# Sinkhorn attention with a feed-forward layer: wider products, products of zeros, and a new order of calls for the first two chunks

## The chip, the cores and the metric

The kernel runs on one core of one Trainium2 chip. The metric is the device time of one launch in microseconds (us), lower is better. TensorE (PE in the profile) multiplies, VectorE (DVE), ScalarE (ACT) and GpSimd (POOL) do the rest, SyncE (SP) only issues transfers (DMAs); POOL and ACT issue some too.

## The reference

```python
P = sort_net                                   # batch 4, 8 heads, 8 x 8 blocks
for _ in range(5):                             # Sinkhorn
    P = exp(P - max(P, -1)); P = P / (sum(P, -1) + 1e-9); P = P / (sum(P, -2) + 1e-9)
k_sorted = einsum('bhij,bhjcd->bhicd', P, k_b) # blocks of 96 positions, head_dim 64
v_sorted = einsum('bhij,bhjcd->bhicd', P, v_b)
attn = softmax(q_b @ k_sorted^T / 8)           # 96 x 96 within each block
x = (attn @ v_sorted) with the heads side by side   # 3072 tokens x 512
h = x @ w_in                                   # 512 -> 2048
out = (h * cos(h)) @ w_out                     # 2048 -> 512
```

All inputs and the output are float32; the kernel multiplies in bfloat16.

## The kernel before

The 3072 tokens are eight chunks of 384: chunk `n` is half of batch `n // 2`, four blocks of 96 tokens numbered `u` = 0 to 3. For each chunk the kernel computes four score tiles (one for each `u`, eight heads), softmax, the products with the sorted V, a transpose to `xT`, and the two feed-forward products: `up` with cosine and gate, then `down`. Before that K and V are sorted: products of K and V with a block matrix made from `P` (`bds`, `bdv`).

Each engine runs its instructions in the order of the calls, so the order written out by hand at the end of the kernel sets everything. The work of chunk 0 and 1 and the sorting of the first batch's K and V are spread over one long list of calls to small helpers (L770 to L962). From chunk 2 on `moe_up` and `moe_down` take slots with calls.

PSUM has two pools: `B` (`big`, three buffers of two banks) and `C` (`acc`, two of one bank). A helper that takes a tile waits until an earlier tile's readers are done.

The helpers, by what they do. `kp`, `ks`: products that sort K (three and six tiles), `k_place`, `kse`: their copies out of PSUM. `v0(z)`: eight products that sort an eighth of V of batch 0, `v0e(z)` its copy; z from 4 on reads `vperm`, which GpSimd's `v_permute` fills in two copies, eighths 4 and 5 first. A product reads 128 columns of `vperm` where a channel has 96, so that the last product of `v0(5)` reads into the second copy. `s_ps`, `s_max`, `s_sub`, `expo`: a score tile, its maximum, the subtraction and the exponential. `p_ps`, `p_ev`: transposes of the exponentials and their copy. `av_products`, `av_norm`: products with V and the division. `x_ps`, `x_ev`: transposes to `xT`. `q_products`, `q_place_half`: transposes of Q. `up_four`, `cos_four`, `gate_four`, `down_four`, `down_out`: the feed-forward layer of chunk 0, over half of its tokens (`h`), four of 16 slices (`g`). `keep_warm(n, tile)`: n products of zeros into a tile that is overwritten afterwards; `idle(n)` the same into a tile of its own.

In `v0` each product has more columns than are kept, and the next overwrites the rest:

```python
w = 2 * NB if t == 7 else 4 * NB          # 64 or 128 columns
nc.tensor.matmul(o[:, t * 2 * NB:t * 2 * NB + w], v_cols(z * 8 + t, z > 3)[:64],
                 bdv[:64].rearrange("p x i -> p (x i)")[:, :w], start=True, stop=True)
```

In chunk 2 `expo(2, u)` sends its exponentials through a transposing DMA on SP's queue (unless told to leave that to PE), `down(n, ts, half, stores)` computes 128 tokens of the output in two halves of eight products, copies them to `o_s` and stores them, also through SP's queue. `p_hold(2, 2)` makes GpSimd wait for the transpose of tile (2, 2) before it issues further loads.

The order of calls before, L770 to L963 (several to a line):

```python
v_permute(slice(0, 64), D // 2, False); kp(0, *B); spread(bdv, blocks[1]); kp(2, *B); k_place(0, A); kp(1, *B)
k_place(2, V); v0(0, *C); k_place(1, A); v0(1, *C); v0e(0, V); s_ps(0, 0); v0e(1, A); v0(4, *B); s_max(0, 0)
s_ps(0, 2); load_w_out(0); v0e(4, A); load_w_out(1); load_w_out(2); load_w_out(3); v0(5, *C); ones(0); s_sub(0, 0)
v0(3, *C); v0e(5, A); s_max(0, 2); v0(6, *B); expo(0, 0, True); s_ps(0, 1); s_sub(0, 2); v0e(3, A); p_ps(0, 0, *C)
v0e(6, A); s_max(0, 1); v0(2, *B); p_ev(0, 0, A); s_sub(0, 1); s_ps(0, 3); kxp(1); v0e(2, A); s_max(0, 3)
expo(0, 1, True); v0(7, *B); kxp(0); v0e(7, A); s_sub(0, 3); p_ps(0, 1, *C); kxp(2); z_turned(1); expo(0, 2, True)
av_products(0, 0); p_ev(0, 1, V); expo(0, 3, True); av_norm(0, 0, True); p_ps(0, 2, *B); load(kbuf, 0, kin_d[1])
load(vbuf, 64, vin_d[1]); picks(pick_pair, (2, 3)); av_products(0, 1); p_ev(0, 2, A); p_ps(0, 3, *C)
av_norm(0, 1, True); x_ps(0, 0, *B); q_products(1, 1, 0, 16, *C); x_ev(0, 0, A); p_ev(0, 3, V); x_ps(0, 1, *B)
z_vperm(); av_products(0, 2); q_place_half(1, 1, 0, A); x_ev(0, 1, V); av_products(0, 3); av_norm(0, 2, True)
up_four(0, 0, 0); up_four(0, 0, 1); q_place_half(1, 1, 1, V); z_turned(0); p_pads(); up_four(0, 1, 0)
av_norm(0, 3, True); cos_four(0, 0); up_four(0, 1, 1); gate_four(0, 0); x_ps(0, 3, *C); x_ps(0, 2, *C); cos_four(0, 1)
up_four(0, 2, 0); x_ev(0, 3, V); up_four(0, 2, 1); x_ev(0, 2, A); gate_four(0, 1); up_four(1, 1, 0); cos_four(0, 2)
up_four(1, 1, 1); gate_four(0, 2); up_four(1, 2, 0); cos_four(1, 1); up_four(1, 2, 1); gate_four(1, 1)
up_four(1, 3, 0); cos_four(1, 2); up_four(1, 3, 1); gate_four(1, 2); up_four(1, 0, 0); cos_four(1, 3)
up_four(1, 0, 1); gate_four(1, 3); q_products(1, 0, 0, 16, *C); cos_four(1, 0); last = block(pick_pair, *C)
q_place_half(1, 0, 0, V); up_four(0, 3, 0); q_place_half(1, 0, 1, A); gate_four(1, 0); up_four(0, 3, 1); s_ps(1, 2)
spread(bds[1], last); cos_four(0, 3); s_ps(1, 0); s_max(1, 2); down_four(2, 0); load_q(2)
load_pair(pair, kin_d, 0 * CD // 2, 1 * CD // 2); load_pair(pair, kin_d, 1 * CD // 2, 2 * CD // 2); s_max(1, 0)
v_permute(slice(64, 128)); down_four(2, 1); down_four(2, 2); s_sub(1, 2); down_four(2, 3); gate_four(0, 3)
expo(1, 2, True); ks(2, *C); down_out(2, A); s_sub(1, 0); ks(1, *B); s_ps(1, 1); kse(2, A); p_ps(1, 2, *C)
s_max(1, 1); expo(1, 0, True); s_ps(1, 3); down_four(1, 0); p_ev(1, 2, V); kse(1, A); down_four(1, 1); s_sub(1, 1)
p_ps(1, 0, *B); s_max(1, 3); down_four(1, 2); p_ev(1, 0, A); s_sub(1, 3); av_products(1, 2); expo(1, 1, True)
down_four(1, 3); av_norm(1, 2, True); expo(1, 3, True); p_ps(1, 1, *B); av_products(1, 0); p_ev(1, 1, V)
down_out(1, A); x_ps(1, 2, *C); p_ps(1, 3, *B); av_norm(1, 0, True); x_ev(1, 2, A); av_products(1, 1); down_four(0, 0)
p_ev(1, 3, A); av_norm(1, 1, True); x_ps(1, 0, *C); av_products(1, 3); x_ev(1, 0, V); ks(4, *B); av_norm(1, 3, True)
x_ps(1, 1, *B); down_four(0, 1); x_ev(1, 1, A); kse(4, A); x_ps(1, 3, *B); down_four(0, 2); x_ev(1, 3, V)
down_four(0, 3); ks(0, *B); down_out(0, V); ks(3, *B); kse(0, A); ks(5, *B); kse(3, V); kse(5, A); k_swap(kT[1])
q_transpose(2, 0, (V, V), *B); q_transpose(2, 1, (V, V), *B); zeros_between(3)
```

## Time and profile before

| | |
|---|---|
| median of three runs | 242.27 us (242.16, 242.27, 243.8) |
| profiled execution, its own time | 242.27 us |
| span of its trace | 240.5 us |
| mean granted clock of PE | 0.972 |
| PE busy | 228.5 us (95%) |
| DVE, ACT, POOL busy | 171.8, 153.4, 93.7 us |
| DMA | 30.89 MB, mean 128 GB/s |

The span runs from the first to the last instruction; 1.77 us of the time lie around it. A busy PE is not a PE at its peak: the granted clock says how fast it ran. In the timeline, start and length come first, then engine, line, operation, tile written and tiles read, with the count of instructions; what stands in brackets is the idle time of the engine before it and what ended that. The chain of waits is followed back from the last instruction.

### The profile page before, as it was taken

The page shows a single profiled execution, that of the slowest core. Times are in us where ns is not written, and L with a number is a line of the kernel's source. Part 1 is how long each engine was busy: PE and PEld are TensorE (multiplying, and loading weights), DVE is VectorE, ACT ScalarE, POOL GpSimd, SP SyncE. Part 2 cuts the span into 40 slices and gives each one's busy share as a digit, 9 for nine tenths or more (in the row PEclk, how much of TensorE's full clock was granted, in tenths as well). Part 3 has the DMA queues.
Part 4 walks back from the last instruction along what each step waited for, and adds up shares of the span by engine and source line. Part 5 has one row for each costly group of instructions (what it writes and reads, how often), then busy time and mean ns, then how long its engine had stood idle before and what let it go on. Part 6 is the DMA issues. An engine that isn't in the chain of part 4 may idle for free.

```text
span 240.5 us, 5340 instructions
## 1 busy us (share of the span) xinstructions
PE 228.5 (95%) x2176; PEld 146.3 (61%) x2197; DVE 171.8 (71%) x285; ACT 153.4 (64%) x204; POOL 93.7 (39%) x117
## 2 busy tenths in 40 slices
PE   8888999999999979999999999999999999999993
PEld 3477899666765556655666465655664565456552
DVE  5668766996798656895578986997798769535700
ACT  3366766774889728888488847683767377546511
POOL 7699994893980068960724401700000000000000
PEclk9996579999999999999999999999999999999999
DMA  6999999893899659869798959924982460341012
GB/s 84 212 200 205 203 219 221 118 225 101 141 101 197 144 109 176 127 138 167 103 127 98 117 92 173 182 50 94 118 219 45 85 184 0 68 120 44 3 44 87
DMA packets 66423, 30.89 MB, mean 128 GB/s; under 512 B 55136, under 2 KB 61920, under 8 KB 66144
## 3 DMA queue, kind: packets, MB, share of 16 engines
q0 software_dynamic: 24048, 13.64, 41.3%
q1 hardware_dynamic: 42064, 16.73, 32.5%
q8 instruction: 17, 0.28, 0.5%
q10 hardware_dynamic: 288, 0.20, 0.3%
q14 instruction: 6, 0.05, 0.1%
HBM read 27.27 MB, written 6.29 MB: 140 GB/s over the span
## 4 chain that ended last, share of the span: by engine, by line
PE 74%; DMA 13%; ACT 4%; DVE 3%; POOL 3%; issue 2%; ACTq 0%; DVEq 0%; POOLq 0%
PE h L557 30%; PE o L582 18%; PE h L727 5%; DMA pT<-p_buf 5%; DMA kv<-in_v_dram 5%; PE o L748 4%; PE av L513 3%; PE sc L406 3%; DMA vperm<-p_buf 2%; POOL vperm L179 2%; PE vs L660 2%; PE pps L705 2%; PE ks L376 1%; ACT p_buf L468 1%; DVE s L450 1%
## 5 line engine op out<-in xcount | busy, mean ns | idle before, releaser
L557 PE MATMUL h<-xT,w_in_t 128*128 128x384 bf16 x448 | 78.4, 326 | 0.0
L582 PE MATMUL o<-w_out_t,gg 128*128 128x512 bf16 x303 | 73.6, 379 | 0.9
L565 DVE TENSOR_TENSOR gg<-c,h 128x768 bf16<-128x768 f32 x56 | 52.6, 949 | 18.8 <-ACT c L561 18.8
L561 ACT ACTIVATE c<-h,half_pi 128x768 f32<-128x768 f32 x56 | 50.4, 900 | 22.0 <-PE h L557 21.2
L557 PEld LDWEIGHTS <-w_in_t 128*128 128x128 bf16 x448 | 42.3, 98 | 26.1 <-issue 0.2
L582 PEld LDWEIGHTS <-gg 128*128 128x128 bf16 x320 | 29.0, 98 | 27.6
L179 POOL COPY vperm<-kv 64x1536 bf16<-64x1536 bf16 (+1 forms) x10 | 28.2, 2858 | 0.8 <-DMA kv<-in_v_dram 0.8
L468 ACT ACTIVATE p_buf<-s 96x768 bf16<-96x768 f32 x32 | 25.9, 839 | 2.0 <-DMA pT<-p_buf 0.8
L450 DVE TENSOR_TENSOR s<-sc,mx 96x384 f32<-96x384 f32 (+1 forms) x33 | 24.3, 735 | 1.8
L448 DVE TENSOR_REDUCE mx<-sc 96x4 f32<-96x384 f32 (+1 forms) x33 | 24.1, 729 | 0.7 <-PE sc L406 0.7
L526 DVE TENSOR_TENSOR xn<-av,r 96x512 bf16<-96x512 f32 x32 | 22.0, 687 | 1.1
L524 DVE RECIPROCAL r<-av 96x8 f32<-96x8 f32 x32 | 6.4, 199 | 14.3 <-PE av L513 14.1
L129 POOL DMA_DIRECT2D kv<-in_q_dram x24 | 15.9, 674 | 0.8 <-issue 0.5
L249 ACT CAST kTs<-ks 128x512 bf16<-128x512 f32 (+1 forms) x19 | 11.6, 627 | 7.1 <-PE ks L376 7.1
L406 PE MATMUL sc<-kTs,q_turned 128*128 128x96 bf16 x224 | 15.4, 206 | 0.0
L406 PEld LDWEIGHTS <-q_turned 128*128 128x128 bf16 x224 | 12.7, 98 | 3.6 <-DVE s L450 0.4
L249 ACT COPY kv<-o 128x512 f32<-128x512 f32 x8 | 4.7, 582 | 12.5 <-PE o L582 12.5
L727 PE MATMUL h<-xT,w_in_t 128*128 128x192 bf16 x128 | 12.1, 259 | 0.0
L238 PE MATMUL idle<-warm 128*128 128x512 bf16 x28 | 9.4, 486 | 2.5 <-ACT q_turned L321 1.5
L727 PEld LDWEIGHTS <-w_in_t 128*128 128x128 bf16 x128 | 11.4, 104 | 0.1
L748 PE MATMUL o<-w_out_t,gg 128*128 128x512 bf16 x45 | 11.4, 379 | 0.2
L249 ACT COPY o_s<-o 128x512 f32<-128x512 f32 (+2 forms) x10 | 5.3, 530 | 9.6 <-PE o L582 6.4
(114 smaller groups left out, 282.7 us busy)
## 6 DMA issues: line engine op xcount, KB each, us to landing
...
```

The source lines that it names most:

```text
L179: nc.gpsimd.tensor_copy(dst, src)
L249: eng.copy(dst, src)
L406: nc.tensor.matmul(out, q_of(n, hp)[:, x:x + 128], keys_of(n, u, h2, hp), start=True, stop=True)
L448: nc.vector.reduce_max(mx[:], scv, axis=AX.X)
L450: nc.vector.tensor_tensor(s, scv, mx.to_broadcast(list(s.shape)), op=ALU.subtract)
L468: nc.scalar.activation(p[:, :, :blk], s_t.pop((n, u)).rearrange("p e h c -> p (e h) c"), AF.Exp, scale=scale)
L526: nc.vector.tensor_tensor(xn.rearrange("p h e d -> p e h d"), avv[:, :, :, :D], r.to_broadcast([blk, 2, H2, D]), op=ALU.mult)
L557: nc.tensor.matmul(h[:, f2, :w], w_in_t[:, kk, f * 128:(f + 1) * 128], xT[n][:, kk], start=(kk == 0), stop=(kk == KC - 1))
L561: nc.scalar.activation(c[:], h[:, :, :w], AF.Sin, bias=half_pi[:, 0:1])
L565: nc.vector.tensor_tensor(gt[n, fp // 2][:, f:f + 2], c[:], h[:, :, :w], op=ALU.mult)
L582: nc.tensor.matmul(o[:], gt[n, f // 4][:, f % 4, ts * 128:(ts + 1) * 128], w_out_t[:, f, :], start=(f == 0), stop=(f == FC - 1))
L727: nc.tensor.matmul(o[:, part, f2 * w:(f2 + 1) * w], w_in_t[:, kk, f * 128:(f + 1) * 128], xT[0][:, kk, h * w:(h + 1) * w], start=(kk == 0) ...
```

## The change

Four things. The sorting products of V are up to 192 columns wide on unpermuted V (128 on permuted), and the score products of chunk 0 are 64 wide but for the last of each four. Products of zeros are added: a `fill` argument to `kp`, `v0` and `s_ps`, one of 256 columns in each `p_ps` and `av_products` of chunk 0, two in the fourth Sinkhorn round; in the first round two of four go. The list of calls for chunks 0 and 1 is new: V's eighths come in the order 3, 1, 4, 5, 6, 7, 2, 0, the score tiles in the order 0, 1, 3, 2, the slices of chunk 0's feed-forward layer and its outputs (tokens 0 to 127 first, where 256 to 383 were) come in another order, and five of the six `ks` stand at the end of the list. In chunk 2 the store of tokens 0 to 127 of chunk 1 is held until `expo(2, 2)` has been called, and `av(2, 2)` is called after `down(1, 2, 0)`; in chunk 4's `moe_down`, `expo(5, 3)` is called ahead of `av(5, 0)`.

```diff
@@ -334,12 +334,11 @@
                 ident[:blk, :blk].rearrange("k (r p) -> k p r", r=QR))
             q_twice(0)
             q_twice(1)
-            keep_warm(4, big.tile([128, 512], FP32, name="idle", tag="big"))
+            keep_warm(2, big.tile([128, 512], FP32, name="idle", tag="big"))
         if it >= 2:
             q_place(it - 2)
             if it < 4:
-                if it == 2:
-                    idle(6)
+                idle((6, 2)[it - 2])
                 q_twice(it)
             else:
                 idle(4)
@@ -506,6 +505,8 @@
             xT[n] = xtp.tile([128, KC, TC], BF16, name="xT", tag="xT")
         a = big.tile([128, 2, 512], FP32, name="av", tag="big")
         pt = pT.pop((n, u)).rearrange("p a c -> p (a c)")
+        if n == 0:
+            keep_warm(1, a[:, 0], 256)
         for hp in range(2):
             for h2 in range(H2):
                 e = hp * H2 + h2
@@ -594,7 +595,7 @@
             o_s = op.tile([128, Dm], FP32, name="o_s", tag="o_s")
         late = n > 0 and ts == TC // 128 - 1
         copy_on(V if late else A, o_s[:], o[:])
-        if stores is None:
+        if stores is None or stores == "held":
             kept[n, ts] = o_s
         else:
             store(n, ts, o_s, nc.sync if late else stores)
@@ -626,8 +627,9 @@
 
     ps = {}
 
-    def kp(t, pool, tag):
+    def kp(t, pool, tag, fill=0):
         o = ps["k", t] = pool.tile([128, 16, 2 * NB], FP32, name="ks", tag=tag)
+        keep_warm(fill, o[:, :8].rearrange("p t n -> p (t n)"))
         for z in range(16):
             k_products(o, z, t * 16 + z, slice(64, 128),
                        bds[0][64:, H:].rearrange("p x i -> p (x i)"))
@@ -651,30 +653,34 @@
         copy_on(eng, kT[1][:, ::2, :, t * 8:t * 8 + 8],
                 ps.pop(("ks", t)).rearrange("p t (e m) -> p e m t", e=2))
 
-    def v0(z, pool, tag):
+    def v0(z, pool, tag, fill=0):
         o = ps["v", z] = pool.tile([128, 8, 2 * NB], FP32, name="vs", tag=tag)
-        o = o.rearrange("p t n -> p (t n)")
+        keep_warm(fill, o.rearrange("p t n -> p (t n)"))
         for t in range(8):
 
-            w = 2 * NB if t == 7 else 4 * NB
+            w = min(8 - t, 2 if z > 3 else 3)
             nc.tensor.matmul(
-                o[:, t * 2 * NB:t * 2 * NB + w], v_cols(z * 8 + t, z > 3)[:64],
-                bdv[:64].rearrange("p x i -> p (x i)")[:, :w], start=True, stop=True)
+                o[:, t:t + w].rearrange("p w n -> p (w n)"), v_cols(z * 8 + t, z > 3)[:64],
+                bdv[:64, :H].rearrange("p x i -> p (x i)").unsqueeze(1).to_broadcast(
+                    [64, w, 2 * NB]), start=True, stop=True)
 
     def v0e(z, eng):
         copy_on(eng, vS[0][:, :2 * NB, z * 8:z * 8 + 8],
                 ps.pop(("v", z))[:blk].rearrange("p t n -> p n t"))
 
-    def s_ps(n, u):
+    def s_ps(n, u, fill=0):
         o = ps["s", n, u] = big.tile([128, 2, 512], FP32, name="sc", tag="big")
+        keep_warm(fill, o[:, 0])
         if n == 0:
             for a in range(2 * H2):
                 hp, c = a // H2, (u * H2 + a % H2) * blk
                 for x in range(2):
                     rows = slice(x * D, (x + 1) * D)
+                    m, w = a % H2 * nb + u, HT if a % H2 == H2 - 1 else 64
+                    keys = kT[0][rows, 2 * hp].rearrange("p m t -> p (m t)")
                     nc.tensor.matmul(
-                        o[:, x, a * HT:(a + 1) * HT], q_of(0, hp)[rows, c:c + 128],
-                        kT[0][rows, 2 * hp, a % H2 * nb + u], start=True, stop=True)
+                        o[:, x, a * HT:a * HT + w], q_of(0, hp)[rows, c:c + 128],
+                        keys[:, m * HT:m * HT + w], start=True, stop=True)
             return
         for h2 in range(H2):
             for hp in range(2):
@@ -701,6 +707,8 @@
     def p_ps(n, u, pool, tag):
         p = pb.pop((n, u))
         o = ps["p", n, u] = pool.tile([128, 2 * H2, 128], BF16, name="pps", tag=tag)
+        if n == 0:
+            keep_warm(1, o.rearrange("p a c -> p (a c)").bitcast(FP32), 256)
         for a in range(2 * H2):
             nc.tensor.transpose(o[:blk, a, :blk], p[:, a, :blk], ident[:blk, :blk])
```

The list becomes (several calls to a line):

```python
next(wz); v_permute(slice(0, 64), D // 2, False); kp(0, *B, fill=1); spread(bdv, blocks[1]); kp(2, *B, fill=1)
k_place(0, A); kp(1, *B); k_place(2, V); v0(3, *C, fill=1); k_place(1, A); v0(1, *C, fill=1); v0e(3, V); s_ps(0, 0)
v0e(1, A); v0(4, *B, fill=1); s_max(0, 0); v0(5, *C, fill=1); load_w_out(0); load_w_out(1); v0e(4, A); load_w_out(2)
load_w_out(3); ones(0); s_ps(0, 1); s_sub(0, 0); v0e(5, A); v0(6, *C, fill=1); s_max(0, 1); expo(0, 0, True)
v0(7, *B); s_ps(0, 3); v0e(6, A); s_sub(0, 1); p_ps(0, 0, *C); v0e(7, A); s_max(0, 3); v0(2, *C); expo(0, 1, True)
s_ps(0, 2); s_sub(0, 3); kxp(1); v0e(2, A); v0(0, *B, fill=2); p_ev(0, 0, A); s_max(0, 2); kxp(2); v0e(0, A)
p_ps(0, 1, *C); s_sub(0, 2); kxp(0); z_turned(1); expo(0, 3, True); av_products(0, 0); p_ev(0, 1, V); expo(0, 2, True)
p_ps(0, 3, *C); av_norm(0, 0, True); load(kbuf, 0, kin_d[1]); av_products(0, 1); load(vbuf, 64, vin_d[1])
picks(pick_pair, (2, 3)); p_ev(0, 3, A); p_ps(0, 2, *B); av_norm(0, 1, True); x_ps(0, 0, *B); p_ev(0, 2, A)
q_products(1, 1, 0, 16, *C); x_ps(0, 1, *C); q_place_half(1, 1, 0, V); z_vperm(); x_ev(0, 0, A); av_products(0, 3)
av_products(0, 2); x_ev(0, 1, V); av_norm(0, 3, True); up_four(0, 0, 0); up_four(0, 0, 1); av_norm(0, 2, True)
z_turned(0); p_pads(); up_four(0, 1, 0); cos_four(0, 0); q_place_half(1, 1, 1, V); up_four(0, 1, 1); gate_four(0, 0)
x_ps(0, 3, *C); x_ps(0, 2, *C); cos_four(0, 1); up_four(0, 3, 0); x_ev(0, 2, V); up_four(0, 3, 1); x_ev(0, 3, A)
gate_four(0, 1); up_four(1, 2, 0); cos_four(0, 3); up_four(1, 3, 0); gate_four(0, 3); up_four(1, 2, 1)
up_four(1, 3, 1); cos_four(1, 2); up_four(1, 1, 0); cos_four(1, 3); gate_four(1, 2); up_four(1, 1, 1)
last = block(pick_pair, *C); gate_four(1, 3); cos_four(1, 1); up_four(0, 2, 0); up_four(0, 2, 1); spread(bds[1], last)
gate_four(1, 1); up_four(1, 0, 0); cos_four(0, 2); up_four(1, 0, 1); gate_four(0, 2); q_products(1, 0, 0, 16, *B)
cos_four(1, 0); down_four(0, 0); q_place_half(1, 0, 0, V); q_place_half(1, 0, 1, A); load_q(2)
load_pair(pair, kin_d, 0 * CD // 2, 1 * CD // 2); load_pair(pair, kin_d, 1 * CD // 2, 2 * CD // 2); gate_four(1, 0)
down_four(0, 1); v_permute(slice(64, 128)); s_ps(1, 2); s_ps(1, 0); s_max(1, 2); s_ps(1, 3); down_four(1, 0)
s_max(1, 0); down_four(1, 1); s_sub(1, 2); down_four(1, 2); s_sub(1, 0); expo(1, 2, True); ks(4, *B); down_four(1, 3)
s_max(1, 3); expo(1, 0, True); p_ps(1, 2, *B); down_four(0, 2); down_out(1, A); s_sub(1, 3); p_ev(1, 2, A)
down_four(0, 3); kse(4, V); expo(1, 3, True); av_products(1, 2); down_out(0, V); s_ps(1, 1); p_ps(1, 0, *B)
s_max(1, 1); p_ps(1, 3, *C); p_ev(1, 0, A); down_four(2, 0); s_sub(1, 1); p_ev(1, 3, A); down_four(2, 1)
av_norm(1, 2, True); expo(1, 1, True); down_four(2, 2); av_products(1, 3); x_ps(1, 2, *B); p_ps(1, 1, *C)
av_norm(1, 3, True); x_ev(1, 2, A); av_products(1, 0); p_ev(1, 1, A); down_four(2, 3); av_norm(1, 0, True)
av_products(1, 1); down_out(2, A); x_ps(1, 0, *B); av_norm(1, 1, True); ks(3, *B); x_ev(1, 0, A); x_ps(1, 3, *C)
ks(2, *C); kse(3, A); x_ev(1, 3, V); x_ps(1, 1, *B); ks(1, *B); kse(2, A); x_ev(1, 1, V); ks(5, *B); kse(1, A)
ks(0, *B); kse(5, V); kse(0, A); k_swap(kT[1]); q_transpose(2, 0, (V, V), *B); q_transpose(2, 1, (V, V), *B)
```

```diff
@@ -992,9 +1000,10 @@
     expo(2, 1)
     down(1, 0, 0, nc.sync)
     qk(2, 2)
-    down(1, 0, 1, nc.sync, mid=[(k_sort_g, 0, A, *C)])
+    down(1, 0, 1, "held", mid=[(k_sort_g, 0, A, *C)])
     qk(2, 3)
     expo(2, 2)
+    let_go(1, 0)
     k_sort_g(4, A, *B)
     down(1, 1, 0, nc.sync)
     k_sort_g(8, A, *B)
@@ -1008,10 +1017,10 @@
     v_permute(slice(0, 128))
     down(1, 1, 1, nc.sync)
     k_sort_g(12, A, *B)
-    av(2, 2, True)
     av(2, 1, True)
     p_transpose(2, 3, A, *C)
     down(1, 2, 0, nc.sync)
+    av(2, 2, True)
     x_transpose(2, 1, V, *B)
     av(2, 3, True)
     x_transpose(2, 0, V, *B)
@@ -1061,7 +1070,7 @@
                [(qk_half, 5, 2, 1)], [], [(qk, 5, 3)]])
     expo(5, 1)
     expo(5, 2)
-    moe_down(4, [[(qk, 6, 0)], [(av, 5, 0), (expo, 5, 3)], [(qk, 6, 1)],
+    moe_down(4, [[(qk, 6, 0)], [(expo, 5, 3), (av, 5, 0)], [(qk, 6, 1)],
                  [(av, 5, 2), (expo, 6, 0)], [(av, 5, 3, True), (expo, 6, 1), (qk, 6, 2)]],
              None, mid={3: [(av, 5, 1)], 5: [(x_transpose, 5, 3, A, *B)]})
     q_transpose_dma(7)
```

258 lines of the change are left out of this document (129 added, 129 removed).

## Prediction

> **What bounds the kernel now.** I read the page first. One digit run of its busy slices stands out: the clock granted to TensorE (PE) falls to 5 and 6 tenths in slices four to six, 18 to 36 us.
>
> ```profile
> span 240.5 us, 5340 instructions
> PEclk9996579999999999999999999999999999999999
> ```
>
> Next I asked for busy time and clock by stretch. In a stretch's row stand its length, the busy time of PE, PE's weight loads, DVE, ACT and POOL, then the granted clock. The drop lies at 19.74 and the rise at 33.4, 13.65 us later; I cut the time around it into quarters of that, 3.41 us.
>
> ```profile
> 19.50:19.75 0.25, 0.03 (x1) 0.04 (x2) 0.25 (x2) 0.00 (x0) 0.25 (x2) 0.98 1.23 205
> 33.25:33.50 0.25, 0.25 (x4) 0.24 (x3) 0.22 (x1) 0.00 (x0) 0.25 (x1) 0.72 1.24 201
> 9.50:12.91 3.41, 2.06 (x38) 1.30 (x37) 2.34 (x12) 2.10 (x5) 1.86 (x5) 1.00 1.01 213
> 16.33:19.74 3.41, 2.26 (x60) 2.08 (x60) 3.17 (x5) 1.89 (x3) 3.41 (x3) 1.00 1.24 207
> 19.74:23.15 3.41, 3.41 (x44) 3.08 (x45) 2.57 (x4) 2.61 (x5) 3.41 (x5) 0.50 1.24 206
> 26.57:29.98 3.41, 3.32 (x49) 2.93 (x46) 2.56 (x6) 2.32 (x4) 3.33 (x6) 0.50 1.24 208
> 29.98:33.39 3.41, 3.41 (x36) 3.29 (x35) 2.62 (x6) 2.08 (x2) 3.30 (x5) 0.50 1.25 206
> ```
>
> So for a quarter of the first 60 us PE runs at half clock and is full while DVE has a quarter of its time free: there PE's clock is the bound. Then the chain of waits from 28 us (start, length, what), with six rows of the timeline and the thinnest later stretch:
>
> ```profile
> 17.59 0.95 DVE L692 TENSOR_REDUCE mx<-sc 96x8 f32<-96x768 f32 x1 [0.21 <-PE sc L675]
> 19.72 0.23 PE L660 MATMUL vs<-bdv,vperm 64*128 64x64 bf16 x1 [1.16 <-POOL vperm L179]
> 31.24 3.84 PE L727 MATMUL h<-xT,w_in_t 128*128 128x192 bf16 x32
> 35.08 0.34 PE xps L714 x8
> 35.42 6.60 PE h L727 x80
> 42.02 0.49 PE qps L260 x16
> 42.51 0.30 PE bl L361 x8
> 48.84 0.34 PE sc L406 x8
> 51.63 0.36 PE pps L705 x8
> 52.86 0.26 PE av L513 x8
> 45.01 11.34 POOL L179 COPY vperm<-kv 64x1536 bf16<-64x1536 bf16 x4 [0.25 <-DMA kv<-in_v_dram]
> 57.16 0.48 ACT L249 COPY xT<-xps 128x384 bf16<-128x384 bf16 x1 [1.18 <-PE xps L714]
> 58.16 1.73 PE o L748 x8
> 59.89 0.25 PE ks L376 x8
> 60.16 0.59 ACT kTs L249
> 60.80 1.07 PE qps L260 x32
> 165.00:170.00 5.00, 4.65 (x39) 2.37 (x38) 3.81 (x7) 2.95 (x5) 0.00 (x0) 1.00 0.55 103
> ```
>
> From 31.24 to 60.8 the chain is PE after PE, with one wait (0.6 us, for the last `kse`). Behind that PE is full but for one gap, at 84.2 to 85.7.
>
> **Why the clock fell, as far as the rows show.** Busy time doesn't say it: the stretch from 9.50 was busy 2.06 us and kept its clock, that from 16.33 was busy 2.26 and lost it. Columns streamed, weighted by the rows that an operand fills, do better.
>
> ```profile
> 9.05 1.47 PE L238 MATMUL idle<-warm 128*128 128x512 bf16 x6 [0.18 <-ACT q_turned L321]
> 12.73 1.03 PE L238 MATMUL idle<-warm 128*128 128x512 bf16 x4 [1.29 <-ACT q_turned L321]
> 10.57 0.87 PE L315 MATMUL qps<-ident,q_mem 96*64 96x96 bf16 x32
> 15.87 1.43 PE L660 MATMUL vs<-bdv,kv 64*128 64x128 bf16 x14
> 17.14 0.41 PE L675 MATMUL sc<-kTs,q_turned 64*128 64x48 bf16 x15
> ```
>
> A product of 512 columns takes 0.21 us ((1.47-0.19)/6, 0.19 being the tail of one), so a stretch has room for 8,190. From 9.50 on stood some 2,400 columns of products of zeros over all rows (30%) and 32 transposes of 96 columns, which by their size add 14%. From 16.33 on stood some 4,500 columns of narrow products over 64 of 128 rows: 28%. So the level below which the clock is lost lies above 28%, and below 30% if transposes count nothing, or 44% if they count by size.
>
> By the Trainium skill ("TensorE: Matmul & The Clock Gate", Part 1) a free-running window of 3.41 us decides; 13.65 us here is four of them, so the trace agrees. Free-running means that another run may cut elsewhere.
>
> **The change, part by part.**
>
> *Before the scores.* In the start-up, products of zeros move from one place (four to two) into the thinnest stretch (two more at the fourth round); PE waits 1.29 us for ScalarE there, so they cost nothing, and if that cover were gone 0.43. Each `kp` and the early `v0` get one product of 512. The first `kp`'s lies in the 0.17 us that PE waits for `spread` (0.05 stays); the second's and those of two `v0` are 0.64. Products of `v0` on unpermuted columns go from 128 to 192 columns: they take 0.102 us each now (1.43/14), where 192 columns stream in 0.08; so 0 to 0.027 each over twelve, I take 0.1 in all, as the weights pace them. The first score tile is ready 0.8 us later: `s_max(0,0)` at 18.4 instead of 17.59. The wider score products (48 to 64 columns) are paced by their weights too: 0.
>
> *The 1.16 us wait for GpSimd.* The last product of `v0(5)` reads into the second copy, in before and after alike; that copy ends at 19.7. But PE now comes to it later: from 18.4 it has `v0(4)` and `v0(5)`, 16 products at 0.08 and two fills, 1.65 us, so to 20.05. The wait goes, the stretch before 19.74 is full, and by my count of columns it has 53% where it had 28%.
>
> *Does the clock then hold?* 19.74 to 26.6 holds five fills of 512, the wide products, four scores' worth and the first fills of 256: some 42%. The thin one is 26.6 to 30.0, mostly transposes: 2,450 weighted columns of fills and `av` products are 30%, with transposes by size 55%. Both are at or above what held before, so I take full clock throughout.
>
> *The chain of chunk 0 at full clock.* DVE sets it first: four maxima and four subtractions, at
>
> ```profile
> L696 DVE TENSOR_TENSOR s<-sc,mx 96x768 f32<-96x768 f32 x4 | 3.8, 954 | 0.2
> L692 DVE TENSOR_REDUCE mx<-sc 96x8 f32<-96x768 f32 x4 | 3.8, 952 | 1.2 <-PE sc L675 1.2
> 25.34 0.95 DVE L696 TENSOR_TENSOR s<-sc,mx 96x768 f32<-96x768 f32 x1
> ```
>
> Eight of them are 7.6 us: 18.4 to 26.0, where before ended at 26.29, having waited 1.2. From the exponential of tile 3 (about 26.4: two of 0.85 follow the last `v0e`) PE has two `p_ps` (0.36), three `av` (0.26), two `x_ps` (0.17), `q_products` (0.49) and five fills of 256 columns (0.107): 2.9 us, so `up_four` starts at 29.3 if nothing waits (the lower bound), and at 30.4 if `p_ev`, `av_norm` and `x_ev` each arrive last. I take 29.9. Before: 31.24, and its first 2.15 us ran at half clock, worth 1.07.
>
> *From there to the first transposes of chunk 2.* PE's work is the same in both: 128 products of `up_four` 10.56 (6.60/80 each), `x_ps` 0.34, `q_products` 0.49, `block` 0.30, 48 of `down_four` 10.38 (1.73/8), and four each of scores, `p_ps`, `av` and `x_ps` with six `ks` at the rows above 6.0: 28.1 us. Before: 31.24+28.1+1.07 = 60.4, measured 60.80, so 0.4 of waits. After: the new list ends with five `ks`, and behind the last `down_four` ScalarE has `down_out` and `x_ev` and four `kse` (0.59+0.48+4x0.59 = 3.4 us) where PE has 2.1: up to 1.3 of waiting, 0 if DVE's turn comes early; I take 1.0. 29.9+28.1+1.0 = 59.0: **1.8 us gained** (bounds: 29.3 without a tail, 57.4, gains 3.4; 30.4 with 1.3, 59.8, gains 1.0). GpSimd's copies of V, 45.0 to 56.4 by a DMA, still end before they are wanted.
>
> *Chunk 2: held store, later `av(2,2)`.*
>
> ```profile
> 79.74 0.84 ACT L468 ACTIVATE p_buf<-s 96x768 bf16<-96x768 f32 x1
> 80.61 0.53 SPq L572 DMA_DIRECT2D out_dram<-o_s  x1
> 81.25 1.27 SPq L481 DMA_TRANSPOSE pT<-p_buf  x1
> 85.70 0.68 PE L513 MATMUL av<-vS,pT 96*128 96x65 bf16 x16 [1.53 <-DMA pT<-p_buf]
> 85.78 0.18 POOL L485 CAST held<-pT 96x1 f32<-96x1 bf16 x1 [14.78 <-DMA pT<-p_buf]
> 166.86 0.43 PE L513 MATMUL av<-pair,vperm 96*128 96x65 bf16 x8 [0.29 <-DMA vperm<-p_buf]
> ```
>
> The exponential of `(2,2)` is done at 80.58, but its transpose goes out at 81.25, behind the store on SP, and lands at 85.7. Without the store ahead it goes out 0.6 earlier; and `av(2,2)` now stands behind `av(2,1)`, `p_transpose` and eight `down` products, 2.4 us further down. So PE's wait of **1.53 us** goes (0.9 to 1.6: something of it may come back at `x_transpose`). What waits behind: on SP the store behind the transpose, whose buffer is wanted again only 10 us later; on GpSimd the loads behind `p_hold`, which go out 0.6 us or more earlier. At 163 the transpose of `(5,3)` passes one of `xT`: the 0.29 us wait goes, **0.3**.
>
> After 90 us PE is idle for 0.35 us at most in any 5 (the stretch from 165), so what is won stays won. Sum: 1.8+1.5+0.3 = 3.6. The profiled execution took 242.27 (span 240.5 and 1.77 around it), which is the median too: 242.3-3.6 = **238.7**.
>
> **The rivals.**
>
> *R1: the transposes' stretch loses the clock.* If transposes count nothing, 26.6 to 30.0 has 30% against a level between 28 and 30%. Then 30.0 to 33.4, all `up_four`, runs at half clock, as it did in before, and the rise comes at its end: 1.7 us, 240.4. For it: 26.57 to 29.98 was nearly all transposes and didn't raise the clock although PE was busy 3.32 of 3.41. Against: by size it's 55%. The Trainium skill ("TensorE: Matmul & The Clock Gate", Part 4) has transposes not counted as busy in the same way; that rule gives this rival.
>
> *R2: the clock falls near 20 us as before, and the added products run at half clock.* Behind 19.74 the list adds 3,584 columns of zeros (7 times 0.43 = 3.0 us), 768 of width (0.64) and a fourth score tile (0.65), less 0.4 of idle time filled: `up_four` at 35.1. If the clock is up by then, PE comes to chunk 2's transposes at 35.1+28.1+1.0 = 64.2 against 60.8, and with 1.8 won later the time is 243.9: slower. It decides if the drop comes with two or more stretches still at half clock. For it: 80 narrow products and 16 transposes still stand there. Against: 53% where the drop came from 28%.
>
> *R3: the clock holds, but the gap at 84 us comes back* as waits for `x_transpose` or chunk 1's tail takes 1.3 and more: gains 1.8-0.6 and 0.6, about 240.5.
>
> **Chances.** Forecast 0.58, R1 0.20, R2 0.12, R3 0.10. The range goes from 236.9 (the bounds' 3.4+1.6+0.3 would be 237.0) to 242.0, which takes in R1 and R3 and leaves out R2. A measurement of this kernel tells about 1% from no change (239.85 and 244.7). Faster: most of the forecast, a third of R1 and R3, 0.62. Slower: R2 with the rise a stretch late (1.7 more), and what I haven't seen, 0.10. Within: 0.28.
>
> **What would show it.** Clock by stretch at 1.00 from 16 to 36 us; no wait of PE for GpSimd's copy; `up_four` from about 29.9, the transposes of chunk 2's queries from about 59; no wait of `av` near 83. A clock of 0.5 in one stretch is R1, in more R2. I am wrong if DVE's eight end well after 26.0, if the tail of chunk 1 waits over 1.5 us, or if the gain at 59 is gone at 100.

## The result and the profile after

The kernel after takes 241.39 us (median of 14 runs, 240.15 to 243.27), the kernel before on the same chip 242.23 (14 runs): a ratio of 0.9951, 95% interval 0.9931 to 0.9972. That is 1.2 us less (0.7 to 1.7) where 3.6 were forecast; the two medians alone differ by 0.8. Ratios leave out executions far above the others of their kernel: 816.32 of `thin_zeros` (the execution that was profiled, so its twin `thin_look` stands in for it), 244.34 of `thin_256`, 244.00 and 246.19 of `no_256`, and 466.80 and 245.97 of before. The profiled execution took 240.86 us with a span of 239.1; before had 242.27 and 240.5, so the two traces differ by 1.4.

The page of the kernel after has no drop of the clock left (the digits are the granted clock in tenths, 9 is 90% or more):

```profile
span 239.1 us, 5377 instructions
PEclk9999999999999999999999999999999999999999
```

The same quarters as before (length, busy time of PE, weight loads, DVE, ACT, POOL, then granted clock):

```profile
16.33:19.74 3.41, 3.41 (x50) 2.60 (x46) 2.30 (x3) 1.60 (x2) 3.41 (x3) 1.00 1.24 207
19.74:23.15 3.41, 3.41 (x73) 2.74 (x71) 3.34 (x5) 2.94 (x6) 3.41 (x5) 1.00 1.24 206
26.57:29.98 3.41, 3.22 (x71) 2.82 (x69) 3.20 (x9) 3.35 (x6) 3.30 (x7) 1.00 1.24 208
29.98:33.39 3.41, 3.41 (x50) 3.41 (x48) 3.00 (x6) 2.32 (x3) 3.33 (x4) 1.00 1.24 205
```

PE is full from 16.33 to 23.15; in the first of these quarters it was busy for 2.26 us before. In 26.57 to 29.98 it does 71 products where it did 49. The timeline of the kernel after (start, length, what; in brackets the idle time of the engine ahead of it and what ended that), at the places of the prediction's steps:

```profile
19.12 0.95 DVE L698 TENSOR_REDUCE mx<-sc 96x8 f32<-96x768 f32 x1 [0.71 <-PE sc L681]
25.80 0.95 DVE L702 TENSOR_TENSOR s<-sc,mx 96x768 f32<-96x768 f32 x1
29.98 2.22 PE L735 MATMUL h<-xT,w_in_t 128*128 128x192 bf16 x25
57.40 0.58 ACT L249 COPY o_s<-o 128x512 f32<-128x512 f32 x1 [1.28 <-PE xps L722]
58.04 0.39 PE L375 MATMUL ks<-bd,kv 128*128 128x64 bf16 x8 [0.70 <-ACT o_s L249]
58.25 2.08 ACT L249 CAST kTs<-ks 128x512 bf16<-128x512 f32 x4
59.89 0.88 PE L260 MATMUL qps<-ident,q_mem 96*64 96x96 bf16 x32 [0.30 <-ACT kTs L249]
83.54 1.89 PE L583 MATMUL o<-w_out_t,gg 128*128 128x512 bf16 x8
86.71 0.34 PE L545 MATMUL xps<-order,xn 96*128 96x96 bf16 x4 [0.59 <-DVE xn L527]
89.18 1.46 PE L558 MATMUL h<-xT,w_in_t 128*128 128x384 bf16 x8
141.09 0.43 PE L514 MATMUL av<-pair,pT 96*128 96x65 bf16 x8 [0.91 <-DMA pT<-p_buf]
143.94 2.28 PE L558 MATMUL h<-xT,w_in_t 128*128 128x384 bf16 x13
167.95 2.27 PE L558 MATMUL h<-xT,w_in_t 128*128 128x384 bf16 x13 [0.18 <-DMA xT<-xn]
```

Against the rows of before, `up_four` begins 1.26 us earlier (31.24 there) and chunk 2's Q transposes 0.91 (60.80). The rows of before for the later places are these:

```profile
91.24 0.98 PE L557 MATMUL h<-xT,w_in_t 128*128 128x384 bf16 x5
142.39 0.42 PE L513 MATMUL av<-pair,pT 96*128 96x65 bf16 x8
```

So the lead is 2.06 us where chunk 2's `up` begins (91.24 and 89.18), but 1.30 at the last `av` of chunk 4 (142.39 and 141.09). Time was lost at three places, in the waits at 58, 87 and 141 us.

### The profile page after: what moved, and what is told of

It is laid out like the page before. It is cut to its first block, busy times and chain, and to the rows that moved or that the text cites. A ratio compares the mean times of both kernels' runs of the same rounds, so it can differ in the third digit from the quotient of the medians.

```text
span 239.1 us, 5377 instructions
## 1 busy us (share of the span) xinstructions
PE 227.4 (95%) x2191; PEld 143.9 (60%) x2214; DVE 171.1 (72%) x284; ACT 153.9 (64%) x205; POOL 93.6 (39%) x117
## 4 chain that ended last, share of the span: by engine, by line
PE 81%; DMA 6%; ACT 5%; DVE 3%; issue 3%; POOL 1%; SPq 0%; ACTq 0%; POOLq 0%
PE h L558 31%; PE o L583 22%; PE h L735 4%; PE o L756 4%; PE sc L405 3%; DMA pT<-p_buf 3%; PE av L514 3%; PE vs L662 2%; PE ks L375 2%; PE vs L425 1%; ACT p_buf L467 1%; DMA vperm<-p_buf 1%; PE pps L713 1%; DMA xT<-xn 1%; PE xps L545 1%
## 5 line engine op out<-in xcount | busy, mean ns | idle before, releaser
L558 PEld LDWEIGHTS <-w_in_t 128*128 128x128 bf16 x448 | 42.2, 98 | 26.5 <-issue 0.6
L249 ACT CAST kTs<-ks 128x512 bf16<-128x512 f32 (+1 forms) x18 | 10.9, 637 | 6.4 <-PE ks L375 6.4
L129 POOL DMA_DIRECT2D q_mem<-in_q_dram x16 | 10.7, 691 | 1.3 <-DMA kv<-in_v_dram 1.0
L735 PE MATMUL h<-xT,w_in_t 128*128 128x192 bf16 x128 | 11.1, 246 | 0.0
L238 PE MATMUL idle<-warm 128*128 128x512 bf16 x28 | 8.7, 450 | 2.4 <-ACT q_turned L321 1.4
```

The costliest lines, as they stand in the source:

```text
L129: nc.gpsimd.dma_start(out=q_heads[:, i, :, e], in_=src[:, ih * IC + i, :, e])
L249: eng.copy(dst, src)
L558: nc.tensor.matmul(h[:, f2, :w], w_in_t[:, kk, f * 128:(f + 1) * 128], xT[n][:, kk], start=(kk == 0), stop=(kk == KC - 1))
```

## What delays the transposes

Rows of the traces that I had not looked at explain most of it. The list of DMA queues has one named `instruction` (packets, MB, share of 16 engines); in the kernel after, and in before alike:

```profile
q8 instruction: 17, 0.28, 0.5%
```

These are packets of 16 KB. The 0.5% is the time of 16 engines together, so a packet takes about 1.1 us of one engine's time; that it holds up more than that one engine no row shows. PE has 2,214 products and 2,214 weight loads, one packet for each 260 of these 4,428, and with more PE instructions at the start the packets come earlier (experiments below), so I take them for PE's program arriving, in blocks. The Trainium skill ("Runtime: NRT & Kernel Launch", section on instruction fetch mechanics) has an engine's program arrive in 16 KiB blocks of 256 instructions and calls the cost of crossing from one to the next mostly hidden. The size agrees. What PE itself loses there no run here shows; the delay that I mean falls on other transfers. The DMA view of a window (a transposing transfer's row ends with its median us from issue to landing) for the transpose of tile (2, 2), first in before (81.2 to 85.7 us), then in `b_pad` (82.2 to 85.1), the kernel before with more PE instructions at its start, where no block came:

```profile
q8 instruction: 1, 0.02, 1.4%
pT<-p_buf SPq DMA_TRANSPOSE x1, 4.4
...
pT<-p_buf SPq DMA_TRANSPOSE x1, 2.8
```

and for tile (4, 3) in the kernel after, 136.5 to 141.1:

```profile
q8 instruction: 1, 0.02, 1.3%
pT<-p_buf SPq DMA_TRANSPOSE x1, 4.5
```

A transpose of this kind takes 2.8 us where no block of instructions comes, and 4.4 or 4.5 in these two, where one comes while it is under way. In before a block fell at 83.4, onto tile (2, 2), for which PE waited 1.53 us from 84.2. The next one that bears on this, at 141.4, came 2.3 us into the transpose of tile (4, 3), which landed after 2.8 us all the same. In after the blocks fall at 79.2 and 139.0: the first delays tiles that are wanted later, the second, 2.45 us into its transpose, tile (4, 3), for which PE waits 0.91 us. The 17 products that the change adds in all are 34 PE instructions: every later block comes that much earlier in the program.

## The experiments

Ratios are to the kernel before on the same chip. "Waits" are PE's of 0.35 us or more in the profiled execution.

| kernel | median us | ratio (95%) | span | waits of PE behind 55 us, at us |
|---|---|---|---|---|
| `again` | 241.74 | 0.9941 (0.9910-0.9973) | 240.1 | 0.42 at 57.8, 0.59 at 86.4, 0.54 at 111.3, 1.67 at 140.2 |
| `thin_zeros` | 245.81 | 1.0082 (1.0050-1.0114) | | |
| `thin_look` | 245.66 (one run) | | 243.9 | 0.59 at 90.5, 1.01 and 0.36 at 142.9 |
| `thin_256` | 241.07 | 0.9915 (0.9881-0.9948) | 238.3 | 0.59 at 85.8, 0.77 at 140.3 |
| `third_out` | 240.54 | 0.9886 (0.9842-0.9930) | 239.4 | 0.60 at 85.8, 1.13 and 0.45 at 138.4 |
| `x_first` | 241.09 | 0.9933 (0.9904-0.9962) | 239.3 | 0.50 at 87.4, 1.14 and 0.53 at 138.4 |
| `late_only` | 242.10 | 0.9976 (0.9948-1.0005) | 240.8 | 0.59 at 88.9, 0.39 at 209.5 |
| `early_only` | 241.44 | 0.9956 (0.9932-0.9980) | 239.6 | 0.50 at 57.8, 1.28 at 84.2, 0.92 at 141.5 |
| `start60` | 241.14 | 0.9908 (0.9873-0.9942) | 239.3 | 1.26 at 64.6, 0.40 at 81.5, 0.59 at 87.8, 0.43 at 208.4 |
| `b_start60` | 246.29 | 1.0111 (1.0069-1.0153) | 242.8 | 1.11 and 0.40 at 140.2, 1.85 at 169.1 |
| `b_shift34` | 243.02 | 1.0022 (0.9999-1.0045) | 240.6 | 0.98 at 85.2, 0.71 at 142.5 |
| `b_pad` | 242.90 | 1.0004 (0.9981-1.0027) | 239.5 | 0.78 at 66.2 |
| `pad` | 241.04 | 0.9940 (0.9915-0.9965) | 240.0 | 0.56 at 58.3, 0.39 at 64.9, 0.59 at 87.5, 0.43 at 207.9, 1.01 at 211.1 |
| `pad_third` | 240.58 | 0.9921 (0.9891-0.9951) | 238.6 | 0.88 at 64.8, 0.59 at 87.4 |
| `no_256` | 241.06 | 0.9933 (0.9901-0.9964) | 238.7 | 0.59 at 86.1, 0.36 at 110.4, 0.77 at 140.7 |
| `best3` | 240.88 | 0.9926 (0.9902-0.9950) | 239.2 | 0.59 at 85.7, 0.85 at 110.5, 1.01 at 141.1 |

**The products of zeros.** `thin_zeros` and `thin_look` are one kernel; `thin_256` thins the eight products in `p_ps` and `av_products` alone (its expectation names `up_four` where `p_ps` is meant).

```diff
-        keep_warm(fill, o.rearrange("p t n -> p (t n)"))          # and in kp
+        keep_warm(fill, o.rearrange("p t n -> p (t n)"), 2)
-            keep_warm(1, a[:, 0], 256)                             # and in p_ps
+            keep_warm(1, a[:, 0], 2)
```

> The changed kernel with every added product of zeros in the first two chunks' list cut to 2 columns (512 or 256 before); the count of instructions stays. Theory, the zeros hold the clock: the granted clock falls to 0.5 near 20 us for two to four stretches of 3.41 us, the first up_four starts at 32 us or later (29.98 in the changed kernel), and the time is 1.5 to 4 us above the changed kernel's, so above the kernel before too. Rival, the order and the wider products hold it alone: clock 1.00 throughout, up_four at 29 to 30, time within 0.5 us of the changed kernel.

> The changed kernel with all its added products of zeros cut to 2 columns, looked at once more for the clock by stretch. Theory: without those columns the granted clock falls at a point between 15 and 20 us and stays at 0.50 to about 33 us, up_four's first products run at half speed, and chunk 2's Q transposes come 3 to 4 us later than in the changed kernel. Rival: the clock stays at 1.00, and the lost time is elsewhere.

> The changed kernel with the products of zeros in av and up_four (256 columns each) cut to 2 columns; the 512-column ones of chunk 0 stay. If the columns of 18 to 24 us alone carry the clock past the stretch of Q transposes (26.6 to 30.0 us), the granted clock stays at 1.00 to 60 us and the time is that of the changed kernel, or 0.2 us less for the columns saved. If that stretch needs them (the first rival of my prediction), the clock stands at 0.50 from 27 to 30 us on for some microseconds, up_four's first products take twice their time, and the time is 1.5 to 2.5 us above the changed kernel.

With two columns each the kernel is slower than before. Its clock by stretch, `up_four` and chunk 2's Q transposes, from `thin_look`:

```profile
19.74:23.15 3.41, 3.03 (x54) 2.86 (x55) 2.61 (x4) 2.44 (x5) 3.41 (x6) 0.50 1.24 206
33.39:36.80 3.41, 3.41 (x25) 3.23 (x24) 1.71 (x5) 0.90 (x1) 3.33 (x3) 0.53 1.29 231
32.80 4.62 PE L735 MATMUL h<-xT,w_in_t 128*128 128x192 bf16 x32
63.63 0.88 PE L260 MATMUL qps<-ident,q_mem 96*64 96x96 bf16 x32
```

The clock falls, `up_four` starts 2.8 us later than in after and the Q transposes 3.7. So the columns of zeros hold the clock, and the new list without them would have cost time. In the profile of `thin_256` the 512-column ones do it alone: the quarter before `up_four` kept its clock

```profile
26.57:29.98 3.41, 3.04 (x69) 2.68 (x70) 3.21 (x10) 3.38 (x6) 3.33 (x6) 1.00 1.24 208
```

and the time is not above that of after. My count gave that quarter 30% with the fills and without transposes; without its five fills of 256 columns 1,170 of the 2,450 weighted columns are left, 14%. If transposes counted nothing, and if that quarter was one window, the clock should have been lost. The Trainium skill's rule behind R1 ("TensorE: Matmul & The Clock Gate", Part 4: transposes are not counted as busy in the same way) is thus not borne out by this one profile. It is not refuted either. Where the window lay in that execution is not known, and the mean clocks of single executions speak for the 256-column products: 0.993 or less, as one stretch of 3.41 us at half clock would give, stands in 5 of 26 executions of the kernels without them (one of 8 of `thin_256`, four of 12 of `no_256`, none of 6 of `best3`) and in 3 of 78 of those with them (one of the 14 of after, at 243.27 us, and two of `x_first`).

**The tail of chunk 1.** In after PE waits 0.70 us at 57.3 for ScalarE's copy into the third output tile of chunk 0; there are two such buffers, and the first store lands late. `third_out` puts that tile into a free buffer of the cosine pool.

```diff
-        o_s = op.tile([128, Dm], FP32, name="o_s", tag="o_s")
+        if ts == 2:
+            o_s = cosp.tile([128, 2, TC], FP32, name="c", tag="c").rearrange("p a c -> p (a c)")[:, :Dm]
+        else:
+            o_s = op.tile([128, Dm], FP32, name="o_s", tag="o_s")
```

> The changed kernel, with the third output tile of chunk 0 copied into a buffer of the cosine pool instead of the output pool, which has two. Theory, ScalarE's copy at 57.4 waits until the first of the three stores, sent at 49.2, has landed: the copy starts at about 56.5, PE's wait of 0.70 us before the next sorting products of K goes, chunk 2's first transposes come 0.5 to 0.8 us earlier (59.1 to 59.4 for 59.89), and the time falls by as much. Rival, the four kse on ScalarE rule the end of the list: chunk 2's first transposes come less than 0.2 us earlier and the time doesn't change.

The wait goes and the Q transposes come at 58.98, 0.91 earlier. But the store alone can do as much. The DMA view's row of the first store in after and then in `x_first` (last column: us from issue at 49.2 to landing), and the copy and the Q transposes in `x_first`:

```profile
out_dram<-o_s SPq DMA_DIRECT2D x1, 256.0 KB, 8.1
out_dram<-o_s SPq DMA_DIRECT2D x1, 256.0 KB, 7.2
56.53 0.58 ACT L249 COPY o_s<-o 128x512 f32<-128x512 f32 x1 [0.40 <-DMA out_dram<-o_s]
59.02 0.88 PE L260 MATMUL qps<-ident,q_mem 96*64 96x96 bf16 x32
```

In five profiles in which the copy waits for it (after, `again`, `start60`, `x_first`, `thin_256`) the store landed at 57.30, 57.02, 56.48, 56.43 and 56.23, and the Q transposes came at 59.89, 59.61, 59.07, 59.02 and 58.95: 2.6 to 2.7 us behind. The gain in time is not settled (below). Why the store takes 7.0 us in one execution and 8.1 in the next stays open.

**The same kernel twice.**

> The changed kernel itself, unaltered, for a second profile and as the yardstick of the others on one chip. My reading: where the lost time sits is set by the program and not by chance, so this profile again has no gap at 84, a wait of 0.6 us for the x_transposes near 86.7, a wait of 0.9 us for a probability transpose near 141 and PE instructions fetched at 79, 94, 107, 122 and 139 us; time 0.993 to 0.997 of before. Rival: the late landing of the first store of chunk 0 (8.1 us) and of the transpose at 141 (4.5 us against 2.8) are chances of one execution, so here one of them is missing.

The reading held for the places, 58, 86.4 and 141 us, and not for the size: here the wait in chunk 4 is larger, and a new one stands at 111.

```profile
111.32 0.61 PE L425 MATMUL vs<-bd,vperm 128*128 128x128 bf16 x8 [0.54 <-ACT pair L249]
140.18 0.43 PE L514 MATMUL av<-pair,pT 96*128 96x65 bf16 x8 [1.67 <-DMA pT<-p_buf]
```

The block of instructions came at 137.8 instead of 139.0, onto tiles (4, 2) and (4, 3). So which transfer a block meets is set by the program within 1.2 us in these two executions, and chance does the rest: spans of 239.1 and 240.1 for one kernel.

**The later calls.** `late_only` is before with the edits in chunks 2 and 4 alone, `early_only` is after without them.

```diff
-    down(1, 0, 1, nc.sync, mid=[(k_sort_g, 0, A, *C)])
+    down(1, 0, 1, "held", mid=[(k_sort_g, 0, A, *C)])    # and let_go(1, 0) behind expo(2, 2)
-    av(2, 2, True)                                        # ahead of av(2, 1); now behind down(1, 2, 0)
-    moe_down(4, [[(qk, 6, 0)], [(av, 5, 0), (expo, 5, 3)], ...
+    moe_down(4, [[(qk, 6, 0)], [(expo, 5, 3), (av, 5, 0)], ...
```

> The kernel before with only the later calls: the store of chunk 1 held, av(2, 2) later, expo(5, 3) ahead of av(5, 0); no zeros, no new list. Theory: PE's instructions are fetched while the transpose of tile (2, 2) is under way, which makes the gap of 1.53 us at 85.7; called later the product does not wait, but the x_transposes wait 0.6 us for the PSUM buffer as in the changed kernel: up(2, 0) 0.9 us earlier, the swap another 0.3 us, time 1.0 to 1.2 us below before. Rival, as in my prediction: the whole 1.53 and 0.3 stay won, time 1.8 us below. Second rival: with the transposes of chunk 4 in another place against the fetch, 0.9 to 1.5 us are given back near 141 and the time is that of before within 0.3 us.

> The changed kernel without the later calls: store of chunk 1 at once, av(2, 2) in its old place, expo(5, 3) behind av(5, 0). Theory: a block of instructions comes near 79, while the transposes of tiles (2, 1) and (2, 2) are under way; av(2, 2) in its old place waits for it by 0.7 to 1.4 us, no wait for x_transpose; the wait near 141 stays; time 0.4 to 1.0 us above the changed kernel, 0.997 to 1.000 of before. Rival, as in my prediction: half of the gain is the first two chunks', so 1.8 us below before; or the later calls bring nothing and the time is the changed kernel's within 0.3 us.

```profile
88.92 0.34 PE L544 MATMUL xps<-order,xn 96*128 96x96 bf16 x4 [0.59 <-DVE xn L526]
```

is the wait that `late_only` has in place of the 1.53, and these are two rows of `early_only`, SP's store of chunk 1 and the product that waits:

```profile
79.32 1.74 SPq L573 DMA_DIRECT2D out_dram<-o_s  x1
84.16 0.68 PE L514 MATMUL av<-vS,pT 96*128 96x65 bf16 x16 [1.28 <-DMA pT<-p_buf]
```

There the block at 79.2 delays the transposes ahead, SP needs 1.74 us for the store where before it needed 0.53, and the transpose of (2, 2) goes out at 81.17, late. Without the later calls PE waits 1.28; with them it waits 0.59 in another place. In the time that is little: `early_only` alone has 0.9956, all of it 0.9951 and 0.9941 (`again`), and `late_only` has 0.9976 with an interval that reaches 1: 0.6 us below before, where I had expected 1.0 to 1.2. My expectation for `early_only` (0.997 to 1.000) was too high; by these medians most of the gain is the first two chunks', but intervals of 0.2 to 0.3% either way don't exclude a half. `late_only` has the clock against it too: none of its twelve executions has a mean clock above 0.963, where 12 of 30 of before on the same chip have 0.97 or more.

**The wait for x_transpose.**

```diff
+    x_transpose(2, 1, V, *B)
+    x_transpose(2, 0, V, *B)
     av(2, 2, True)
-    x_transpose(2, 1, V, *B)
     av(2, 3, True)
-    x_transpose(2, 0, V, *B)
```

> The changed kernel with x_transpose(2, 1) and x_transpose(2, 0) called ahead of av(2, 2) and av(2, 3). If the 0.59 us wait near 86.7 is for one of the three big PSUM buffers that av(2, 2), av(2, 3) and a transpose hold, it goes, every later milestone comes 0.6 us earlier, and the time is 0.6 us below the changed kernel. Rival: the buffers are short whatever the order, so av(2, 2) or av(2, 3) waits instead by 0.4 to 0.6 us, and the time is the changed kernel's within 0.2 us; if the transposes of xn wait for the vector engine's product itself, the wait moves ahead and grows.

```profile
87.36 0.33 PE L545 MATMUL xps<-order,xn 96*128 96x96 bf16 x4 [0.50 <-DVE xT L251]
```

It doesn't go, it moves to a later transpose, and the time is that of `again`: the rival held in the time, though the wait came at a transpose and not at an `av`. My reading is that the two last `av` of the chunk, DVE's division and the transposes behind it are too close together for what PE has between them; no run tests that further.

**Moving the blocks.** Each of these changes PE's count of instructions in the start-up alone: 45 more products and loads (`start60`, `b_start60`), 17 (`b_shift34`, as many as the change adds), 87 (`pad`, `b_pad`; `pad_third` with the third output as above: by the profiles' counts 29 products are cut, not 28).

```diff
-    keep_warm(15, big.tile([128, 512], FP32, name="idle", tag="big"))
+    keep_warm(60, big.tile([128, 512], FP32, name="idle", tag="big"), 128)   # start60, b_start60
+    keep_warm(32, big.tile([128, 512], FP32, name="idle", tag="big"), 240)   # b_shift34; pad: all 29 in four
```

> The changed kernel, with 60 start-up products of zeros of 128 columns instead of 15 of 512: the same columns, 90 instructions of PE more, so that PE's fetches of instructions (one per 256) fall 90 instructions earlier in the program. Theory, a fetch that falls into a transposing DMA delays it from 2.8 to 4.0 to 4.5 us: the fetch at 139.0 moves to about 130, the transpose of tile (4,3) takes 2.8 to 3.0 us, the wait of 0.91 us at av(4,3) goes, and the time falls by 0.5 to 0.9 us unless another fetch falls into a transpose that is waited for. Rival, earlier loads crowd the DMA engines there: the transpose of (4,3) still takes over 4 us, time within 0.3 us of the changed kernel.

> The kernel before with the same 60 start-up products of 128 columns for 15 of 512 and nothing else. Theory of the fetches: the one at 83.4 moves to about 74, the transpose of tile (2,2) takes about 2.8 us instead of 4.4 though the store still stands ahead of it, PE's wait of 1.53 us at 85.7 shrinks to 0.2 or less, and the time falls by 0.8 to 1.5 us, less if another transpose that is waited for is hit. Rival, the prediction's reading: the store ahead of it on the queue makes the transpose late, the wait stays at 1.3 to 1.6 us, time as before.

> The kernel before with 32 products of 240 columns at its start in place of 15 of 512: as many columns, but 17 products and 17 weight loads more, as many as the change adds in all. Theory: each later instruction block comes 34 instructions, about 1.9 us, earlier; the one at 141.4, which meets no awaited transfer, comes near 139.5 and delays the transposes of tiles (4, 2) and (4, 3): a wait of 0.8 to 1.7 us opens before up(4, 0), the one near 85.7 stays between 1.0 and 1.6 us, and the time is 0.8 to 1.7 us above before. Rival: the wait at 141 in the changed kernel comes of its order of calls, so none opens here and the time is that of before within 0.4 us.

> The kernel before with its 28 start-up products cut into four each in the same way, nothing else. Theory: the block that came at 83.4 comes near 76 and the one at 141.4 near 133, so the wait of 1.53 us at 85.7 goes with no call moved, and up to 1 us opens in chunk 4; if the clock falls at 20 us as before, the time is 0.5 to 1.5 us below before; if it falls at 16 or 17 us, as in the other kernel with a cut start, 1 to 4 us above. Rival: the wait at 85.7 belongs to the order of calls and stays at 1.0 to 1.6 us.

The last three hold the order of calls of before and change nothing but PE's count at the start. PE's products of tile (2, 2) and of the last tile of chunk 4 in `b_start60`, `b_shift34` and `b_pad`, two rows each:

```profile
85.07 0.68 PE L513 MATMUL av<-vS,pT 96*128 96x65 bf16 x16 [0.18 <-DMA pT<-p_buf]
140.23 0.43 PE L513 MATMUL av<-pair,pT 96*128 96x65 bf16 x8 [1.11 <-DMA pT<-p_buf]
```

```profile
85.22 0.68 PE L513 MATMUL av<-vS,pT 96*128 96x65 bf16 x16 [0.98 <-DMA pT<-p_buf]
142.51 0.43 PE L513 MATMUL av<-pair,pT 96*128 96x65 bf16 x8 [0.71 <-DMA pT<-p_buf]
```

```profile
85.12 0.55 PE L513 MATMUL av<-vS,pT 96*128 96x65 bf16 x12
141.38 0.42 PE L513 MATMUL av<-pair,pT 96*128 96x65 bf16 x8
```

Blocks at 79.5 and 137.7: the first wait goes, the second opens. At 80.3 and 140.4: 0.98 and 0.71. At 76.4, 86.6, 130.2 and 143.6, between the transposes: neither, though no call was moved. So both the wait that the later calls were to remove and the one that the change got in its place follow the count of PE's instructions.

The median follows less well. `b_pad`'s profile was the shortest of twelve executions, and its median is that of before. Its eleven other executions have mean clocks of 0.955 to 0.964, where 11 of 27 of before on that chip have 0.97 or more, so its median carries a longer half clock. In `b_shift34`'s profile the waits are 1.69 us together against 1.53, and the time is 0.4 us above before, not 0.8 to 1.7. `b_start60` came slower than I expected of it, by 1.1% against before: its waits of 3.5 us, where before has 1.8, give 1.7 of the 2.7 us, and the rest is open. The longer half clock of its profile (last section) is no reason: the mean clocks of its executions, 0.958 to 0.972, are in the range of before on that chip, 0.954 to 0.972. In `start60` the block comes at 131.3, the wait at 141 is gone, as it should be, and one of 1.26 opened at 64.6, where a block at 62.1 met the copy of `kTs` (4.4 us to land, 2.9 in after).

> The changed kernel with each of its 28 start-up products of 512 columns cut into four of 128: 84 products and 84 weight loads more, all before 14 us. Theory: every later block of PE's instructions then comes 168 instructions (7 to 10 us) earlier, between 122 and 134 us and near 59 and 70 us, where no awaited transpose is under way: the waits near 64, 111 and 141 are at most 0.3 us each, the clock stays at 1.00, and the time is 0.8 to 1.6 us below the changed kernel (0.988 to 0.991 of before). That would be the larger part of what my prediction missed. Rival: the blocks meet other transfers that are awaited, waits of 1 us or more open elsewhere, and the time is the changed kernel's within 0.4 us.

> The same with the third output tile of chunk 0 in a buffer of the cosine pool, so that nothing on the scalar engine waits for the first store near 57. Theory: 0.2 to 0.8 us below pad (0.985 to 0.989 of before), chunk 2's Q transposes at 59.0. Rival: the store lands in time anyway, time that of pad.

```profile
64.78 0.33 PE L405 MATMUL sc<-kTs,q_turned 128*128 128x96 bf16 x4 [0.88 <-ACT c L562]
```

```profile
211.11 0.43 PE L514 MATMUL av<-pair,vperm 96*128 96x65 bf16 x8 [1.01 <-DMA vperm<-p_buf]
```

The first row is `pad_third`'s, the second `pad`'s. The waits at 111 and 141 are gone in both, as expected. But `up_four` begins later with the cut start (30.42 and 30.63), and the blocks meet others: at 61 the copy of `kTs` (3.9 us to land in `pad_third`; the scalar engine, named as releaser, had long been done) and, in `pad`, a transpose of chunk 7 (4.8 us). The wait near 64 was to be 0.3 at most; it is 0.88 in `pad_third`. The theory of the blocks held; that the forecast's time would nearly come with them out of the way did not.

**Fewer products.**

```diff
-            keep_warm(1, a[:, 0], 256)      # and the one in p_ps
```

> The changed kernel without its eight 256-column products of zeros (four in the evictions' stretch of p, four in av of chunk 0); the nine 512-column ones stay. Theory: PE's instruction stream is read in blocks of 256, and a block's arrival delays a transposing transfer that is under way; with eight products and eight weight loads fewer every later block comes 16 instructions, some 0.9 us, later against the transfers, so the block near 139 just misses the transpose of tile (4, 3): the wait near 141 falls from 0.8 to 1.7 us to at most 0.4 us, the clock stays at 1.00, and the time is 0.6 to 1.5 us below the changed kernel. Rival: the wait at 141 belongs to the new order of calls, and stays at 0.8 to 1.7 us; then the time is the changed kernel's, or 0.2 us less.

> no_256 with the third output tile of chunk 0 in a buffer of the cosine pool. Theory: the copy on the scalar engine near 57 does not wait for the first store to land (7.0 to 8.1 us), so the Q transposes of chunk 2 start at 59.0 whatever the store does, against 59.0 to 59.9; 0 to 0.6 us below no_256. Rival: the 7 us landing was already short enough, time that of no_256.

The rival held. Eight products fewer were too few: the block still came at 138.6 and 139.0, tile (4, 3) took 4.4 and 4.6 us, and a wait at 110 came on top. Both are about 0.7% below before; neither is told apart from after. The lowest ratio of all is `third_out`'s, but the two other kernels with its edit have 0.9921 and 0.9926, and on `third_out`'s chip before itself took 243.57 us and had a mean clock below 0.97 in 11 of 16 executions. So its worth over after, 0 to some 1 us, is not settled.

## Why the prediction was wrong

The two profiled executions account for it, as far as two executions can: the medians differ by less than they do. Forecast 3.6, got 1.4; missing are 0.9 (tail of chunk 1), 0.6 (chunk 2), 0.9 (chunk 4) and 0.2 (the swap), and 0.4 came in small gains elsewhere.

- **The clock: right.** 1.00 through all stretches of the profile, by the products of zeros. R1 and R2 did not come there; one of the 14 executions (0.992) lost about a stretch of 3.41 us.
- **The GpSimd wait: right.** PE is full from 16.33 to 23.15.
- **DVE's chain: too early, and made up for.** `s_max(0, 0)` came at 19.12 and not 18.4. The chain of waits of after has three fills ahead of the scores, at 0.32 each where I took 0.21:

```profile
15.16 0.32 PE ks L238
...
16.52 0.32 PE vs L238
...
17.68 0.32 PE vs L238
```

  That is 0.96 of the 1.53 us by which it came later; the rest I have not traced. DVE's eight ended at 26.75, not 26.0, yet `up_four` began at 29.98, where I had 29.9: from DVE's end to there it took 3.2 us and not 3.9. That the start came out right is luck: two errors of 0.7 us cancel.
- **The tail of chunk 1: the term that was mis-sized.** I took 1.0 of waits for "`down_out` and `x_ev` and four `kse`" on ScalarE, from durations. By my own 28.1 us of work, 29.98 to 59.89 leaves 1.8: PE waits 0.70 for that copy and 0.30 for the last `kse`, and most of the rest is that its work took more than I summed (it is busy for 28.76 us). I had not asked what the third output's copy needs: one of two buffers, whose first store lands 7.0 to 8.1 us after its issue. The 1.8 us of gain were there where the store landed early (`x_first` and `thin_256`, Q transposes at 59.02 and 58.95), 0.9 in the profile of after. Even there my 1.0 fits by luck: in `x_first` PE is busy for 28.63 of these 29.02 us, so it was work and hardly waiting for ScalarE.
- **The gap at 84: the right wait, the wrong cause.** I read it as "behind the store on SP". The store cost 0.6 of the way, but the transpose took 4.4 us instead of 2.8, and without that delay there is no wait: `b_pad` has store and order of before, and no gap. The 1.53 went; 0.59 came back at `x_transpose`, which I had named as a possibility in the term and as R3.
- **The swap:** the wait of 0.29 went, and PE then waits 0.18 for `xT` at 167.95.
- **"What is won stays won": the step that failed outright.** I looked only at where PE is idle in before. The wait at 141 is not in before's trace: the change makes it, by moving a block of instructions onto a transpose. It was there in every profile of a kernel with the change's instructions and its start-up uncut (0.77 to 1.67 us, two waits in three of them), and not in before, `late_only` and `b_pad`. With the start-up cut, so that the blocks fall elsewhere, it went (`start60`, `pad`, `pad_third`), and the order of before got it by such a cut alone (`b_start60`, `b_shift34`).

R3 came nearest (240.5): part of the gap back as the wait for `x_transpose`, the tail longer than I took. It did not have the wait at 141.
